# Block sums made in place by accumulating DMAs, with signs turned where the blocks are made, and products that wait for one part

## The chip, the cores and the metric

The kernel runs on one core of one Trainium2 chip. The metric is the device time in microseconds of one execution. The engines are TensorE (PE, matmuls), VectorE (DVE), ScalarE (ACT), GpSimd (POOL) and SyncE (SP, which here only issues DMAs).

## The reference

Talking-heads attention is followed by two feed-forward stages. Inputs and output are float32 in value; the weights arrive as float64 words and are decoded on the core.

```python
scores = scale * q @ k.T;  scores = einsum('bhij,hg->bgij', scores, w_pre)
attn   = softmax(scores);  attn   = einsum('bhij,hg->bgij', attn, w_post)
x      = (attn @ v)                      # 1792 tokens x 768
h      = ((x @ w1) * (x @ w2)) @ w3      # d_ff = 1024
x2     = h @ w_out                       # 1792 x 768
r      = maximum(x2 @ w_in, 0)           # d_ff = 2048
out    = (r * r) @ w_out2                # 1792 x 768
```

The change lies between the last matmuls of x2 and those of x2 @ w_in.

## The kernel before

Precision is kept by splitting each float32 operand into a high and a low half in float16. A product of two blocks is three matmuls (high by high, high by low, low by high), and a "cast" below always means two instructions: ScalarE writes the high half, VectorE the low half as the scaled source less the high half (lines 1434 and 1430 for x2, 1124 and 1125 for the weights).

**x2 and its sums.** w3 and w_out are multiplied into one matrix M first. The loop over four column blocks of 448 tokens (`for i in range(B)`) makes x2 as 24 products of 24 matmuls each; each result is evicted by ScalarE (line 1710) into a tile of the 16-buffer ring `st`. Two successive blocks form one half `t` of x2, cut into four blocks b11, b12, b21, b22 of three tiles each. x2 @ w_in is done by Winograd's form of Strassen's method: seven products instead of eight, of the sums T1 = b12 - b11, T2 = b22 - T1, T3 = b22 - b12, T4 = b21 - T2 on this side. `x2_steps(t, ts)` (line 1654) makes them by subtractions on GpSimd (line 1658) and casts the seven operands.

**The weights' sums.** w_in is taken in eight pairs q of two row blocks. `form_in` (line 1061) loads the two blocks of a pair from DRAM, where the decoding has put them (`sides`, line 1066: x0 = A11, A12 and x1 = A21, A22, tiles `ib`), and makes S1 = A21 + A22, S2 = S1 - A11, S3 = A11 - A21, S4 = A12 - S2 on GpSimd (line 1073) into two tiles `it` (pairs 0 to 2) or four tiles of `st`. `ib` and `it` share a ring of four buffers: a pair takes all four. The seven blocks are then cast into one tile `wq` (two buffers; pair 0 has a place of its own). For pairs 3 and up the casts wait until the pair two before has been used for both halves of tokens (`over`).

**The products.** The main loop runs over SEQ, sixteen steps of pair and half: (0,0), (1,0), (2,0), (1,1), (2,1), (0,1), (3,0), (3,1), (4,0) and so on. In each step `multiply_in` (line 1840) does seven block products of nine matmuls in the order A11, [S1 of the step before], S3, A12, S2, [S4 of the step before], A22. Its first line, `need_in(q)`, makes sure that the whole pair's operands have been written down in the program. What the engines then wait for are semaphores on the parts that they read.

**The order of the work** is set by a planner that runs when the program is built. Each helper is a stream of steps (engine, planned cost, function); `tick` moves a planned clock on by what PE does and lets each stream, in the order of a list, issue its next steps as long as its engine's planned backlog stays small (`ahead`). A REST step holds a stream for a planned time, `after(eng)` until an engine's backlog is worked off. This fixes only the order in each engine's queue: instructions, DMA issues included, run in order on their engine.

The accumulating DMA is issued by GpSimd. In the kernel before, GpSimd issues DMAs only for scales that cross partitions (lines 806 and 809): `across <- tot` to DRAM, and `ac <- across` back.

Of the kernel before, what the change touches and what calls it, by code (L numbers as in the profile page):

```python
# [10 lines left out]
F32 = mybir.dt.float32  # L11
# [3 lines left out]
ALU = mybir.AluOpType  # L15
# [19 lines left out]
def talking_heads_attention_moe_moe2(  # L35
# [726 lines left out]

    def decode(raw, n, total=None, x=None, zt=None):
# [189 lines left out]
    def one_steps(i):  # L953
# [15 lines left out]
        if kind in ("in", "out"):  # L969
            sums = in_sums[:, j : j + 1] if kind == "in" else out_sums[j // OG][:, j % OG : j % OG + 1]  # L970
            x, ops = decode(t, n, sums)
            yield from read_raw(i, x, ops)
# [25 lines left out]

    in_w, x_of, over = {}, [], set()
    fin_pool = []  # L1000

# [55 lines left out]
    def have_scale(g):  # L1057
        need(("in", (g + 1) * IG - 1))
        finish(scaling[g])

    def form_in():

        for g in range(NF2 // IG):
            box = {}

            def sides(q):
                box["b"] = [flat(w_tile(1, "ib")) for _ in range(2)]
                flush("kept")
                for z in range(2):
                    nc.sync.dma_start(box["b"][z], kept_in[2 * q + z])  # L1070

            def mix(o, a, b, op=ALU.subtract):
                nc.gpsimd.tensor_tensor(o, a, b, op=op)

            for q in range(g * IG // 2, (g + 1) * IG // 2):
                while ("in", 2 * q + 1) not in wsp:
                    yield REST, 0.5, lambda: need(("in", 2 * q + 1))
                yield POOL, 0, lambda: sides(q)
                yield REST, 5.0, None
                x0, x1 = box["b"]  # L1080
                if q < 3:
                    ta, tb = (flat(w_tile(1, "it")) for _ in range(2))
                    sums = [ta[:, :OH], ta[:, OH:], tb[:, :OH], tb[:, OH:]]
                else:
                    while x_of[1] in streams:
                        yield REST, 0.5, lambda: finish(x_of[1])
                    sums = [stage()[:, :OH] for _ in range(4)]
                a11, a12, a21, a22 = x0[:, :OH], x0[:, OH:], x1[:, :OH], x1[:, OH:]
                for o, l, r, op in (
                    (sums[0], a21, a22, ALU.add), (sums[1], sums[0], a11, ALU.subtract),  # L1090
                    (sums[2], a11, a21, ALU.subtract), (sums[3], a12, sums[1], ALU.subtract),
                ):
                    yield POOL, 1.1, lambda: mix(o, l, r, op)
                while g not in in_scales:
                    yield REST, 0.5, lambda: have_scale(g)
                up, lo = in_scales[g]
                if q:
                    while not started or (q > 2 and q - 2 not in over):
                        yield REST, 0.5, lambda: None
                    w = fin_pool[0].tile([P, 2, 7, OH], F16, tag="wq", name="wq", bufs=2)  # L1100
                    ks = [w[:, :, k] for k in range(7)]

# [3 lines left out]
                else:  # L1106
                    ws = [w_tile(0).rearrange("p z (k o) -> p z k o", k=2) for _ in range(4)]
                    ks = [ws[k][:, :, z] for k, z in ((0, 0), (0, 1), (1, 0), (2, 0), (2, 1), (3, 0), (3, 1))]

                    def where(k, n):  # L1110
                        i, y = ((0, 0), (0, 1), (1, 0), (2, 0), (2, 1), (3, 0), (3, 1))[k]
                        return [ws[i][:, z, y : y + n].rearrange("p k o -> p (k o)") for z in range(2)]

                srcs = [(x0, 0, 2), (x1[:, OH:], 2, 1)]
                if q < 3:
                    srcs += [(ta, 3, 2), (tb, 5, 2)]
                else:
                    srcs += [(x, 3 + k, 1) for k, x in enumerate(sums)]
                parts = [(x, k, where(k, n)) for x, k, n in srcs]
                for x, k, (h, l) in parts:  # L1120
                    n = x.shape[-1] // OH
                    if k == 3:
                        yield after(POOL)
# [4 lines left out]
                in_w[q] = (ks, lo)  # L1128

    forming, started = [], []  # L1130

    def need_in(q):
        if q and not started:
            started.append(True)
        while q not in in_w:
            assert forming[0].step(True) or q in in_w
        return in_w[q]

# [389 lines left out]

    mlo = {}
    M16, wo_done = [], []  # L1530

    def scale_m(o, acc):
# [36 lines left out]
        def scale():  # L1569
            ps = box.pop("ps")  # L1570
            up, mlo[o] = pow2(ps[:, :1], 14, "ms")
            nc.vector.tensor_scalar(rows2[:, o, 1], rows[:, 0], up, None, op0=ALU.mult)
            nc.vector.tensor_copy(bound[:, o : o + 1], ps[:, 1:2])
            if o:
                nc.vector.tensor_reduce(bound[:, 2:3], bound[:, :2], axis=AX.X, op=ALU.max)
                x_scale.append(pow2(bound[:, 2:3], 12 - 15, "xs"))

        yield DVE, 0.45, own
# [75 lines left out]
    def x2_steps(t, ts):  # L1654
        box = {}

        def mix(o, a, b):
            nc.gpsimd.tensor_tensor(o, a, b, op=ALU.subtract)

        def mixes(c):  # L1660
            b11, b12, b21, b22 = ts[c], ts[NDC + c], ts[c + 3], ts[NDC + c + 3]
            box[c] = {B11: b11, B21: b21, B22: b22, T1: b11, T2: b22, T3: b12, T4: b21}
            t1, t2, t3, t4 = (box[c][k] for k in (T1, T2, T3, T4))
            return [
                (POOL, 1.25, lambda: mix(t1, b12, b11)), (POOL, 1.25, lambda: mix(t3, b22, b12)),
                (POOL, 1.25, lambda: mix(t2, b22, t1)), (POOL, 1.25, lambda: mix(t4, b21, t2)),
            ]

        def casts(c, ks):
            yield from casts_of(t, c, [(k, box[c][k]) for k in ks])  # L1670

        if t:
            finish(first_of[0])
            while not fin_pool:
                yield REST, 0.5, lambda: None
        sums = [mixes(c) for c in range(3)]
        for c in range(3):
            yield from casts(c, (B21, B22) if t else (B11, B21, B22))
            if t == 0:
                yield from sums[c]  # L1680
                yield after(POOL)
                yield from casts(c, (T3, T2, T4, T1))
            elif c:
                yield from sums[c - 1]
        if t:
            yield from sums[2]
            for k in (T3, T2, T4, T1):
                for c in range(3):
                    yield from casts(c, (k,))

    have_x, first_of = [set(), set()], []

    def casts_of(t, c, ks):
        yield from halves_steps(
            [([xop(t, z, k, c) for z in range(2)], x, x_scale[0][0]) for k, x in ks]
        )
        for k, _ in ks:
            have_x[t].add((k, c))

    forming.append(Stream(form_in()))  # L1700
    streams.append(forming[0])
    for i in range(B):
# [3 lines left out]
        for c in range(NDC):  # L1706
            pt = mm()
            product(pt, [(M16[f], cols_of(c), hs[f]) for f in range(NFC)], toks(i))
            t = stage()
            nc.scalar.activation(t, pt[:, :S], AF.Copy, scale=mlo[c // 3])  # L1710
            ts.append(t)
            if c < NDC - 1 or i % 2 == 0:
                tick(1.13, 0.65)
        if i == 2:
            first_of.append(Stream(chain(*(casts_of(1, c, [(B11, ts[c])]) for c in range(3)))))
            streams.append(first_of[0])
# [4 lines left out]
    finish(x_of[0])  # L1721
    need_in(0)
    mid.close()
# [110 lines left out]
    xt, zt_, st_, s4_ = {}, {}, {}, {}  # L1834
    A11, A12, A22, S1, S2, S3, S4 = range(7)

# [456 lines left out]
```

## Time and profile before

| | |
|---|---|
| median of three runs | 1231.47 us (1230.94 to 1232.87) |
| the profiled execution | 1236.24 us, its span 1234.5 us |
| PE busy | 1213.4 us, 98% of the span |
| DVE, ACT, POOL busy | 948.6, 804.5, 581.6 us |
| mean granted TensorE clock | 0.994 of full |
| x2's 24 products | 725 to 836 us |
| x2 @ w_in | 836 to 1037 us |

Times count from the start of the span. "Idle before" is time in which an engine stood still ahead of an instruction, with what released it. The granted clock is a share of 2.4 GHz: 0.50 is the lower of its two levels, 1.2 GHz.

### The profile page before, as it was taken

Reading aid. Unit: us, or ns where it says so; the run is one execution under the profiler, and the core shown is the slowest. Engines: PE = TensorE matmul, PEld = TensorE weight load, DVE = VectorE, ACT = ScalarE, POOL = GpSimd, SP = SyncE. Lnnn points to the kernel's source line nnn. Section 1 sums busy time; section 2 is a strip of 40 time slices with the busy share of each in tenths; the row PEclk is TensorE's granted clock in tenths of the full one; section 3 lists DMA queues with packets and bytes.
Section 4 is the critical chain, followed back from the end, with each engine's and each line's share of the span. In section 5 each row is a group of like instructions: output and inputs, shape, how many; then the busy total and the mean of one; then the engine's idle time right before and its main releaser. Section 6 shows DMA issues by size and latency. Waiting matters only on the chain.

```text
span 1234.5 us, 26238 instructions
## 1 busy us (share of the span) xinstructions
PE 1213.4 (98%) x9904; PEld 749.2 (61%) x9904; DVE 948.6 (77%) x1690; ACT 804.5 (65%) x1620; POOL 581.6 (47%) x569
## 2 busy tenths in 40 slices
PE   7999999999999999999999999998999999999998
PEld 3666776677667655555558975554455555666665
DVE  6888899788889957766665875787578774999783
ACT  6788888888888735655554454567778785765430
POOL 3898788889878600110011211526124423667340
PEclk9999999999999999999999999999999999999999
DMA  6456555655645934755524547263478659565562
GB/s 186 123 156 166 141 146 134 169 128 155 171 114 164 260 98 120 159 143 163 133 94 145 171 146 243 76 207 103 143 269 289 237 169 320 180 189 181 171 201 77
DMA packets 139843, 205.02 MB, mean 166 GB/s; under 512 B 33764, under 2 KB 114788, under 8 KB 139716
## 3 DMA queue, kind: packets, MB, share of 16 engines
q1 hardware_dynamic: 136020, 200.01, 54.7%
q10 hardware_dynamic: 3136, 2.40, 0.8%
q8 instruction: 78, 1.28, 0.5%
q0 software_dynamic: 560, 0.93, 0.4%
q14 instruction: 49, 0.40, 0.1%
HBM read 114.60 MB, written 50.16 MB: 133 GB/s over the span
## 4 chain that ended last, share of the span: by engine, by line
PE 80%; DVE 9%; DMA 5%; ACT 2%; issue 1%; POOL 1%; SPq 0%; ACTq 0%; DVEq 0%; POOLq 0%
PE mm L1243 20%; PE mm L2099 15%; PE mm L1847 13%; PE p L284 10%; PE o L380 9%; PE s L241 5%; PE a L494 5%; DVE x L1430 2%; DMA Bt<-S 2%; PE p L1243 2%; DVE xa L776 1%; DVE xa L779 1%; DVE xa L783 1%; DMA raw<-in_moe_w_dram 1%; DVE wq L1125 1%
## 5 line engine op out<-in xcount | busy, mean ns | idle before, releaser
L1243 PE MATMUL mm<-x,w 128*128 128x448 f16 x1044 | 197.7, 352 | 0.0
L1847 PE MATMUL mm<-x,wq 128*128 128x448 f16 x882 | 172.7, 356 | 5.3 <-DVE wq L1125 3.7
L1243 PEld LDWEIGHTS <-w 128*128 128x128 f16 x1152 | 112.2, 98 | 104.3
L284 PE MATMUL p<-Bt,wpre_k 120*120 120x448 f32 x360 | 159.5, 561 | 4.9 <-DMA Bt<-S 4.2
L2099 PEld LDWEIGHTS <-ao 128*128 128x128 f16 x1176 | 115.0, 98 | 77.1 <-issue 1.2
L380 PEld LDWEIGHTS <-EH 120*112 120x112 f16 (+1 forms) x1440 | 124.9, 130 | 44.6 <-issue 37.1
L1847 PEld LDWEIGHTS <-wq 128*128 128x128 f16 x882 | 86.4, 99 | 87.4 <-DVE wq L1125 4.5
L353 POOL TENSOR_SCALAR EH<-E,st 120x448 f16<-120x448 f32 (+1 forms) x152 | 113.1, 752 | 49.1 <-DVE st L336 37.0
L402 DVE TENSOR_TENSOR ATl<-o,ATh 112x480 f16<-112x480 f32 x180 | 116.0, 645 | 22.3 <-ACT ATh L396 21.6
L306 ACT ACTIVATE E<-p,st 120x448 f32<-120x448 f32 x180 | 116.0, 645 | 22.9 <-DVE st L298 14.2
L396 ACT CAST ATh<-o 112x480 f16<-112x480 f32 x180 | 101.2, 562 | 44.3 <-PE o L380 39.4
L380 PE MATMUL o<-wph,EH 120*112 120x120 f16 x720 | 124.6, 219 | 1.0 <-DVE ATl L402 1.0
L380 PE MATMUL o<-wph,EL 120*112 120x120 f16 x720 | 122.6, 216 | 0.0
L380 PE MATMUL o<-wpl,EH 120*112 120x120 f16 x720 | 122.6, 216 | 0.0
L365 POOL TENSOR_TENSOR EL<-F,EH 120x448 f16<-120x448 f32 (+1 forms) x90 | 104.1, 1157 | 32.8 <-issue 19.9
L298 DVE TENSOR_REDUCE st<-p 120x1 f32<-120x448 f32 x180 | 110.1, 612 | 3.1 <-PE p L284 2.8
L1243 PE MATMUL mm<-h,M 128*128 128x448 f16 x576 | 110.2, 353 | 0.0
L2099 PE MATMUL mm<-x,ao 128*128 128x384 f16 x588 | 96.6, 326 | 1.0 <-ACT st L2113 1.0
L2099 PE MATMUL mm<-ow,ao 128*128 128x384 f16 x588 | 96.0, 326 | 0.0
L380 PEld LDWEIGHTS <-EL 120*112 120x112 f16 x720 | 93.9, 130 | 0.0
L367 DVE SCALAR_TENSOR_TENSOR EL<-E,st,EH 120x448 f16<-120x448 f32 (+1 forms) x90 | 83.6, 929 | 10.9 <-POOL EH L353 10.5
L1243 PEld LDWEIGHTS <-M 128*128 128x128 f16 x576 | 55.9, 98 | 52.0 <-DVE M L1430 0.8
(264 smaller groups left out, 2532.9 us busy)
## 6 DMA issues: line engine op xcount, KB each, us to landing
Bt<-S SPq DMA_DIRECT2D x176, 210.0 KB
raw<-in_moe_w_out_dram SPq DMA_DIRECT2D x24, 768.0 KB
g<-ev SPq DMA_DIRECT2D x64, 224.0 KB
gt<-g SPq DMA_DIRECT2D x56, 256.0 KB
raw<-in_moe_w_in_dram SPq DMA_DIRECT2D x16, 768.0 KB
raw<-in_moe_w_dram SPq DMA_DIRECT2D x14, 768.0 KB
raw<-in_moe_w_dram SPq DMA_DIRECT2D x16, 512.0 KB
kept_out<-xa SPq DMA_DIRECT2D x16, 384.0 KB
```

The lines of the kernel that those rows point to most:

```text
L284: nc.tensor.matmul(pt[: n * H, :S], wpre_k.rearrange("p t g -> p (t g)")[: n * H, : n * H], Bt.pop(u)[: n * H], start=True, stop=True,)
L298: nc.vector.tensor_reduce(nsum[u][:n, 0, j : j + 1], Pp[u][:n, :S], axis=AX.X, op=ALU.max, negate=True)
L306: nc.scalar.activation(e[:n], Pp.pop(u)[:n, :S].rearrange("p (a b) -> p a b", a=EG), AF.Exp, bias=t[:n, 0, j : j + 1], scale=1.0, accum_ou ...
L353: nc.gpsimd.tensor_scalar(seven(EH[u][:n]), Ex[u][:n], inverse(u), 1.0, op0=ALU.mult, op1=ALU.mult)
L365: nc.gpsimd.tensor_tensor(a, f, b, op=ALU.subtract)
L367: nc.vector.scalar_tensor_tensor(a, e, inverse(u), b, op0=ALU.mult, op1=ALU.subtract)
L380: nc.tensor.matmul(pt[:CP, c * n : (c + 1) * n], a[:n, c * CP : (c + 1) * CP], w[:n, :n], start=(i == 0), stop=(i == 2),)
L396: nc.scalar.copy(ATs[s][0][:, :, :, m * NR : m * NR + nr], src)
L402: nc.vector.tensor_tensor(ATs[s][1][:, :, :, a], src, ATs[s][0][:, :, :, a], op=ALU.subtract)
L1243: nc.tensor.matmul(pt[:, :S], w[a][:, cs], x[z][:, sl], start=(c == 0 and i == 0), stop=(c == len(parts) - 1 and i == 2),)
L1847: nc.tensor.matmul(pt[:, :S], w[:, a, c * P : (c + 1) * P], xop(t, b, kb, c), start=(start and c == 0 and m == 0), stop=(c == 2 and m == 2 ...
L2099: nc.tensor.matmul(pt[:, :OH], y[:, a, q * P : (q + 1) * P], ow[g, q][kb][:, w], start=(start and q == 0 and m == 0), stop=(q == NQ - 1 an ...
```

## The change

The sums are no longer made by GpSimd instructions but by DMAs that add a source onto a destination in place. Since these can only add, some blocks are stored with their sign turned: w_in's even row blocks (A11, A12) in the decoding, b11 and b22 in the eviction, and B21 and T2 when they are cast. A turned operand always meets a turned one, so that the products are the same.

The order of the casts changes: A11 and A12, S3, A22, S1, and S2 with S4 in one instruction. x1's first half is loaded a second time, for S3 (`box["s"]`), so that a pair of the first three takes three buffers of the ring instead of four. `need_in(q, k)` makes sure only of the part k. For pairs 3 and up the finishing of x2's sums moves ahead of the loads. The diff, cut to its core:

```diff
+    def accumulate(dst, src):
+        nc.gpsimd.dma_start(dst, src, accum_op=ALU.add)
+    LAND = 4.0
+    PLACE = (0, 1, 2, 3, 5, 4, 6)
@@ form_in
             def sides(q):
                 box["b"] = [flat(w_tile(1, "ib")) for _ in range(2)]
+                box["s"] = (flat(w_tile(1, "it")) if q < 3 else stage())[:, :OH]
...
+                nc.sync.dma_start(box["s"], kept_in[2 * q + 1][:, :OH])
...
+                while q > 2 and x_of[1] in streams:
+                    yield REST, 0.5, lambda: finish(x_of[1])
                 yield POOL, 0, lambda: sides(q)
                 yield REST, 5.0, None
                 x0, x1 = box["b"]
-                for o, l, r, op in (
-                    (sums[0], a21, a22, ALU.add), (sums[1], sums[0], a11, ALU.subtract),
-                    (sums[2], a11, a21, ALU.subtract), (sums[3], a12, sums[1], ALU.subtract),
-                ):
-                    yield POOL, 1.1, lambda: mix(o, l, r, op)
+                yield POOL, 0, lambda: accumulate(s3, x0[:, :OH])
+                yield POOL, 0, lambda: accumulate(x1[:, :OH], x1[:, OH:])
...
+                yield from halves(x0, A11, 2)
+                yield after(DVE)
+                yield POOL, 0, lambda: accumulate(x0[:, :OH], x1[:, :OH])
+                yield from halves(s3, S3, 1)
+                yield REST, LAND, None
+                yield POOL, 0, lambda: accumulate(x0[:, OH:], x0[:, :OH])
+                yield from halves(x1[:, OH:], A22, 1)
+                yield from halves(x1[:, :OH], S1, 1)
+                yield REST, LAND, None
+                yield from halves(x0, S2, 2)
@@ x2_steps
+        else:
+            yield from cast(B11, b11)
+        yield after(DVE)
+        yield from add(b11, b12)
+        yield REST, LAND, None
...
+        yield from cast(B22, b22)
+        yield from add(b12, b22)
+        yield REST, LAND, None
+        yield from cast(B21, b21)
+        yield from add(b22, b11)
+        yield REST, LAND, None
+        yield from cast(T3, b12)
+        yield from add(b21, b22)
+        for k, xs in ((T2, b22), (T4, b21), (T1, b11)):
+            yield from cast(k, xs)
@@ decode (turn is set for w_in's even row blocks)
-                xi, lo, 29, 0, op0=ALU.logical_shift_right, op1=ALU.bitwise_or
+                xi, lo, 29, -(2 ** 31) if turn else 0,
+                op0=ALU.logical_shift_right, op1=ALU.bitwise_or
...
-                xi, hi, -(2 ** 31), xi, op0=ALU.bitwise_and, op1=ALU.bitwise_or
+                xi, hi, -(2 ** 31), xi, op0=ALU.bitwise_and, op1=ALU.bitwise_xor
@@ eviction of x2, and its casts
-            nc.scalar.activation(t, pt[:, :S], AF.Copy, scale=mlo[c // 3])
+            o = c // 3
+            turned = (o == 0) == (i % 2 == 0)
+            nc.scalar.activation(
+                t, pt[:, :S], AF.Copy, scale=mturn[:, o : o + 1] if turned else mlo[o]
+            )
...
+        up = mturn[:, 2:3] if k in (B21, T2) else x_scale[0][0]
@@ multiply_in
-        w = need_in(q)[0][ka]
+        w = need_in(q, ka)
```

## Rows read from the trace of the kernel before

**Rows 1.** The page: busy time and share of PE; the chain, by engine.
```profile
PE 1213.4 (98%) x9904; PEld 749.2 (61%) x9904; DVE 948.6 (77%) x1690; ACT 804.5 (65%) x1620; POOL 581.6 (47%) x569
...
PE 80%; DVE 9%; DMA 5%; ACT 2%; issue 1%; POOL 1%; SPq 0%; ACTq 0%; DVEq 0%; POOLq 0%
```

**Rows 2.** Waits of PE, 720 us to the end: total, times, longest.
```profile
PE mm L1847 <- DVE wq L1125: 3.7, 2, 3.2
PE mm L1847 <- ACT wq L1124: 1.6, 1, 1.6
```

**Rows 3.** PE in order of time: start, length, operation, count, idle before.
```profile
836.14 5.27 PE L1847 MATMUL mm<-x,w 128*128 128x448 f16 x27
...
848.56 0.54 PE L1847 MATMUL mm<-x,wq 128*128 128x448 f16 x2
852.27 6.34 PE L1847 MATMUL mm<-x,wq 128*128 128x448 f16 x25 [3.17 <-DVE wq L1125]
...
864.77 2.15 PE L1847 MATMUL mm<-x,wq 128*128 128x448 f16 x7 [0.50 <-DVE wq L1125]
...
867.36 4.31 PE L1847 MATMUL mm<-x,wq 128*128 128x448 f16 x18
...
871.91 8.31 PE L1847 MATMUL mm<-x,wq 128*128 128x448 f16 x43
```

**Rows 4.** Stretches of 2 us: PE busy, granted clock, DMA share, GB/s.
```profile
852.00:854.00 2.00, 1.73 (x5) 0.50 0.31 115
...
868.00:870.00 2.00, 2.00 (x10) 0.78 1.00 369
```

**Rows 5.** Groups by line: busy us, mean ns, idle before.
```profile
L1658 POOL TENSOR_TENSOR st<-st 128x448 f32<-128x448 f32 x24 | 35.2, 1471 | 63.2 <-DVE x L1430 39.8 <-ACT st L1710 22.2
...
L1430 DVE SCALAR_TENSOR_TENSOR x<-st,xs,x 128x448 f16<-128x448 f32 x42 | 35.4, 895 | 12.0 <-ACT x L1434 12.0
...
L1430 DVE SCALAR_TENSOR_TENSOR h<-st,hs,h 128x448 f16<-128x448 f32 x29 | 18.0, 680 | 4.8 <-ACT h L1434 4.8
```

**Rows 6.** GpSimd in order of time (sums of pairs 0, 2, 3; x2's).
```profile
745.08 1.49 POOL L1073 TENSOR_TENSOR it<-ib 128x384 f32<-128x384 f32 x1 [26.66 <-DMA ib<-kept_in]
...
839.40 15.01 POOL L1658 TENSOR_TENSOR st<-st 128x448 f32<-128x448 f32 x10 [1.78 <-DVE x L1430]
854.37 0.99 POOL L1073 TENSOR_TENSOR it<-ib 128x384 f32<-128x384 f32 x1
...
869.60 1.00 POOL L1073 TENSOR_TENSOR st<-ib 128x384 f32<-128x384 f32 x1 [10.38 <-DMA ib<-kept_in]
```

**Rows 7.** ScalarE in order of time.
```profile
837.27 2.34 ACT L1434 ACTIVATE x<-st,xs 128x448 f16<-128x448 f32 x4
839.51 0.62 ACT L1882 ACTIVATE ev<-mm,sci 128x448 f32<-128x448 f32 x1
840.03 0.93 ACT L1124 ACTIVATE wq<-ib,is 128x768 f16<-128x768 f32 x1
```

**Rows 8.** The crossings' tile: who waited, us, times; issue to landing, us.
```profile
  POOL ac L809: 18.7, 5
...
DMA to landing us min/median/max: 3.7/4.3/5.6
```

**Rows 9.** Tile `it`: casts of 768 columns, ns min/median/max, first and last start.
```profile
L1124 ACT ACTIVATE w<-it,is x2: 922/922/922, 778.5 to 779.4; 128x768 f16<-128x768 f32 x2
L1125 DVE SCALAR_TENSOR_TENSOR w<-it,is,w x2: 1012/1012/1012, 779.6 to 780.6; 128x768 f16<-128x768 f32 x2
```

**Rows 10.** SyncE's issues of the loads for pairs 0 and 3.
```profile
739.15 3.12 SPq L1070 DMA_DIRECT2D ib<-kept_in  x2
...
864.78 0.80 SPq L1070 DMA_DIRECT2D ib<-kept_in  x2
```

**Rows 11.** Two stretches: PE, PEld, DVE, ACT, POOL busy; clock; DMA share.
```profile
836.00:872.00 36.00, 30.74 (x146) 14.80 (x145) 25.75 (x39) 24.96 (x48) 22.65 (x18) 0.91 0.34 112
872.00:1020.00 148.00, 148.00 (x784) 76.54 (x785) 107.02 (x166) 119.80 (x251) 48.22 (x38) 1.00 0.66 224
```

More of the change, by code (lines that the diff above doesn't have):

```diff
@@ L970, in one_steps @@
             sums = in_sums[:, j : j + 1] if kind == "in" else out_sums[j // OG][:, j % OG : j % OG + 1]
-            x, ops = decode(t, n, sums)
+            x, ops = decode(t, n, sums, turn=kind == "in" and j % 2 == 0)
             yield from read_raw(i, x, ops)
@@ L999, in talking_heads_attention_moe_moe2 @@
     in_w, x_of, over = {}, [], set()
+    A11, A12, A22, S1, S2, S3, S4 = range(7)
     fin_pool = []
@@ L1080, in form_in @@
                 x0, x1 = box["b"]
[L1081 to L1088, printed above, removed]
-                for o, l, r, op in (
-                    (sums[0], a21, a22, ALU.add), (sums[1], sums[0], a11, ALU.subtract),
-                    (sums[2], a11, a21, ALU.subtract), (sums[3], a12, sums[1], ALU.subtract),
-                ):
-                    yield POOL, 1.1, lambda: mix(o, l, r, op)
+                s3 = box["s"]
+                yield POOL, 0, lambda: accumulate(s3, x0[:, :OH])
+                yield POOL, 0, lambda: accumulate(x1[:, :OH], x1[:, OH:])
                 while g not in in_scales:
@@ L1100, in form_in @@
                     w = fin_pool[0].tile([P, 2, 7, OH], F16, tag="wq", name="wq", bufs=2)
-                    ks = [w[:, :, k] for k in range(7)]
+                    ks = [w[:, :, k] for k in PLACE]
                     def where(k, n):
@@ L1107, in form_in, with halves @@
                     ws = [w_tile(0).rearrange("p z (k o) -> p z k o", k=2) for _ in range(4)]
-                    ks = [ws[k][:, :, z] for k, z in ((0, 0), (0, 1), (1, 0), (2, 0), (2, 1), (3, 0), (3, 1))]
+                    at_ = ((0, 0), (0, 1), (1, 0), (2, 0), (2, 1), (3, 0), (3, 1))
+                    ks = [ws[at_[k][0]][:, :, at_[k][1]] for k in PLACE]
                     def where(k, n):
-                        i, y = ((0, 0), (0, 1), (1, 0), (2, 0), (2, 1), (3, 0), (3, 1))[k]
+                        i, y = at_[k]
                         return [ws[i][:, z, y : y + n].rearrange("p k o -> p (k o)") for z in range(2)]
[L1114 to L1123, printed above, removed]
+                in_w[q] = (ks, lo)
+                def halves(x, k, n):
+                    h, l = where(PLACE[k], n)
                     yield ACT, 0.5 * n, lambda: nc.scalar.activation(h, x, AF.Copy, scale=up)
@@ L1127, in form_in, with need_in @@
                     )
-                in_w[q] = (ks, lo)
+                    have_w.update((q, PLACE.index(PLACE[k] + i)) for i in range(n))
+                yield from halves(x0, A11, 2)
[8 more added lines that the diff above has]
+                yield from halves(x0, S2, 2)
     forming, started = [], []
-    def need_in(q):
+    def need_in(q, k):
         if q and not started:
             started.append(True)
-        while q not in in_w:
-            assert forming[0].step(True) or q in in_w
-        return in_w[q]
+        while (q, k) not in have_w:
+            assert forming[0].step(True) or (q, k) in have_w
+        return in_w[q][0][k]
     def load_to(n):
@@ L1654, in x2_steps @@
     def x2_steps(t, ts):
[L1655 to L1667, printed above, removed]
@@ L1669, in casts, with cast, add @@
-        def casts(c, ks):
-            yield from casts_of(t, c, [(k, box[c][k]) for k in ks])
+        b11, b21, b12, b22 = (ts[i : i + 3] for i in range(0, 2 * NDC, 3))
+        def cast(k, xs):
+            return casts_of(t, range(3), k, xs)
+        def add(os_, xs):
+            for c in range(3):
+                yield POOL, 0, lambda: accumulate(os_[c], xs[c])
         if t:
             finish(first_of[0])
+        else:
+            yield from cast(B11, b11)
+        yield after(DVE)
@@ L1674, in x2_steps @@
+        yield from add(b11, b12)
+        yield REST, LAND, None
+        if t:
             while not fin_pool:
                 yield REST, 0.5, lambda: None
[L1676 to L1689, printed above, removed]
+        yield from cast(B22, b22)
[8 more added lines that the diff above has]
+            yield from cast(k, xs)
@@ L1714, in talking_heads_attention_moe_moe2 @@
         if i == 2:
-            first_of.append(Stream(chain(*(casts_of(1, c, [(B11, ts[c])]) for c in range(3)))))
+            first_of.append(Stream(casts_of(1, range(3), B11, ts[:3])))
             streams.append(first_of[0])
@@ L1721, in talking_heads_attention_moe_moe2 @@
     finish(x_of[0])
-    need_in(0)
+    for k in range(7):
+        need_in(0, k)
     mid.close()
```

17 lines of the change are left out of this document (8 added, 9 removed).

## The prediction, made before the result was known

> **What bounds the kernel now.** I read the page first. TensorE (PE) is busy 1213.4 of 1234.5 us and the chain that ended last lies on it for 80% [rows 1], so an edit elsewhere moves the time only where PE waits. I then asked who PE waits for from 720 us on, the part that the diff touches: 5.3 us on the weight halves of lines 1124 and 1125, in three waits [rows 2]; the only other one is 1 us long and 180 us later. The list of PE's work in order of time puts the three between 848 and 865 us [rows 3]: inside S3 of pair 1 (3.17 us, ended by VectorE), ahead of A11 of pair 2 (the 1.6 us of ScalarE) and inside it (0.50). Before 846 and after 872 the changed operations never stop PE. After the first of them the granted clock is 0.50, the lower of TensorE's two levels, 1.2 GHz, and it is not back at full 4 us after the last [rows 4]. That is a second price: the 25 matmuls that took 6.34 us take 25 x 0.189 + 0.17 = 4.9 us at full clock (0.189 us each from the 43 in 8.31), and 7 and 18 in 2.15 and 4.31 took 1.4 too much as well. So a wait of this kind costs its length and about 1.4 us.
>
> From 836.14 to the next product, A12 of pair 2 at 871.91, PE did 135 matmuls (15 products of 9), 25.6 us of work in 35.8 us. Even if everything were free, about 9 us can be won, 1 us of the rest being scale transposes. S2 of pair 2 starts at 871.9 + 1.7 = 873.6. I use that moment as the mark, as nothing stops PE behind it for 150 us.
>
> **What goes.** 24 subtractions for x2 on GpSimd (1.47 us each, 35.2 us) and 32 for the input weights leave that engine [rows 5]. VectorE wins too: its 42 casts of x2 take 0.895 us on average, many beside them, where the same form is 0.68 us alone [rows 5], 9 us in all. Before 836 all that is worth nothing: PE is never idle there, and the decoding that gets done sooner isn't waited for. Behind 836 it matters: GpSimd's block of ten subtractions (15.01 us from 839.40) held up those of pair 2 until 854.37 [rows 6], and through them the casts of pair 2; the casts of x2 (four, 2.34 us) stood ahead of pair 1's on ScalarE, which began only at 840.03 [rows 7]. Both old waits come from this, and both should go: S3's halves now stand second in the order, and pair 2's A11 needs only its load.
>
> The sign turns (a constant and an xor in the decode, a negated scale in an eviction, four tiny multiplications ahead of the x2 stage) replace instructions of the same shape, so I put them at nothing; the four cost at most 4 x 0.2 us of VectorE where PE has its 24 products ahead. The wait for one part alone I put at nothing by itself: in the trace PE already ran two S3 matmuls at 848.56 on the high half and stopped only for the low one [rows 3], so parts are waited for separately; what changes is the order in which instructions are written.
>
> **What comes.** 56 accumulating DMAs, issued by GpSimd: 12 for each x2 half, 4 for each of 8 pairs. They cost the issuing engine about 0.56 us each, less than the subtractions, but a dependent one can be issued only when the one before has landed. No row shows an accumulating DMA. The nearest are the scale crossings: GpSimd sat 18.7 us in 5 waits for such a DMA to land, 3.74 us each; with 0.56 us for the issue itself that is 4.3, which is also the median from issue to landing, between 3.7 and 5.6 [rows 8]. Those carry 1 to 128 KB. Here 192 KB are read on both sides, 393 KB in all; at the 369 GB/s that the DMAs reached at share 1.00 [rows 4] that is 1.07 us more. I take 4.3 + 1.1 = 5.4 us a hop, with 3.7 (size free) and 5.6 + 1.1 = 6.7 as ends. An on-chip subtraction was 1.0 to 1.7 us: each link of a chain gets three to five times longer.
>
> A rule of the Trainium skill speaks for shorter hops: "DMA: Bandwidth & Descriptors", section on the anatomy of one DMA on the GpSimd path, puts a DMA at about 2.0 us plus its bytes over 436 GB/s, an estimate of 2.4 us here, with which the whole chain below would be hidden. The crossings disagree (3.7 at the least, at 128 KB and under), and the measurement decides; what the short hop would give is the second rival.
>
> **Where the links lie.** For pair 1, S2 = S1 - A11 is made in x0's place, so only after x0's own cast, and S4 is added on S2. S2 and S4 are cast by one instruction, so S2 too waits for S4's DMA. Pair 2's x1 takes the buffer of pair 1's x0 (four buffers, three now taken per pair), so its load waits for that cast; only then come S1, S2 and S4 of pair 2. One after the other:
> - Pair 1's x0: A11 of the first product ends at 836.1 + 1.7 = 837.8, its eviction (0.62) at 838.5; ScalarE's cast 0.93 [rows 7] and VectorE's 1.01 [rows 9]: 840.4. The four casts of x2 aren't ahead any more, since that stream now rests behind its DMAs.
> - S2 and S4: 2 x 5.4: 851.2. The joint cast, 0.92 + 1.01 [rows 9]: 853.1. PE wants this S2 as its tenth product at 851.4 and waits about 1 us; this wait isn't added, since the chain runs on beside it.
> - Load of pair 2's x1 and of the copy of its first half: GpSimd started 2.8 us after the second issue ended for pair 0 and 4.8 us after the first began for pair 3 [rows 6, 10]; I take 4.0: 857.1.
> - The issue for S3 stands first (0.56), then S1, S2, S4: 3 x 5.4: 873.9. ScalarE's high half 0.92: 874.8.
>
> PE, without waits, wants that S2 as its 17th product at 836.1 + 16 x 1.70 + 1 = 864.3, so it gets there by 866 or 867 and stands 8 us, with 1.4 us of low clock behind it: 876.2 against 873.6. **Sum: +2.6 us.** In hops h the mark is at 849.2 + 5h: equal at 4.9 us, 2.5 us sooner at 4.4, 2.5 later at 5.4; with the ends 3.7 and 6.7 it is -5.9 and +9.1, and the load adds 1 us either way.
>
> Queued behind the waiting instructions: on GpSimd the x2 sums of the second half (first wanted at the fourth step, three steps of 11.9 us after 836); on ScalarE and VectorE evictions emitted behind a cast that waits for its DMA, which hold banks of PSUM but are done before PE comes round to them; on SyncE the stores of g behind pair 2's load. Pairs 3 to 7 I put at nothing: they may be cast once the pair two before is used up, 15 us ahead of their A11 and 22 ahead of their S2, and the chain is 2 + 2 x 5.4 + 2 = 15 us. PE is busy 148.00 of the 148 us there now [rows 11].
>
> **Rivals.** (1) The hop lies between 4.4 and 5.4: the new stop at S2 of pair 2 is just as long as the two it replaces, and the time stays within 2.5 us. For it: the crossings' middle is 4.3, and none is under 3.7. Chance 0.29. (2) Faster: hops of 4.4 or less, since these land on chip where the crossings write or read memory off it. At 4.3 the mark is at 870.7, -2.9 us; at 3.7, -5.9; from 3.0 down PE itself sets it, at 864.3, -9.3. Against it: twice the reading, and neighbours. Chance 0.31. (3) Much slower: hops of 8 us where three x2 transfers (672 KB and as much read again) are ahead in the same queue. The mark moves to 889, +15.6. Against it: only the first hops of each pair have such neighbours, and the DMAs stand at a share of 0.34 in this stretch [rows 11]. Chance 0.10. My own case, hops of 5.4 to about 6.7, has 0.30, so slower has 0.40 in all.
>
> **The numbers.** The profiled execution took 1236.24 us (span 1234.5), 4.8 above the median 1231.47; I add the difference to the median: 1231.5 + 2.6 = 1234.1. About 0.2% (2.5 us) is what can be told from no change. The range, 1226 to 1241, goes from the short hop of 3.7 to the long one of 6.7; the extremes of rivals 2 and 3 stay out. Chances: faster 0.31, same 0.29, slower 0.40; the forecast lies at the edge of the last two.
>
> **What the changed profile would show.** Right: no wait at S3 of pair 1 or A11 of pair 2; one wait of 5 us or more at S2 of pair 2, on ScalarE's cast, whose own wait ends with an accumulating DMA; accumulates 5 to 6 us apart where dependent; x2 casts at 0.68 us. Wrong: a hop under 4.4 us, a load that isn't held by the joint cast, or waits at the fourth step or at pairs 3 to 7.

## The result: 10.5 us slower, half of it at a stop that was foreseen, and priced too low

The changed kernel takes 1242.35 us (median, 1239.74 to 1244.69) against 1231.85 for the kernel before in the same comparison: a ratio of 1.0084, 95% interval 1.0069 to 1.0100, or +10.5 us. The forecast was +2.6, with 1241 as the upper end of the range. The profiled execution took 1243.43 us, its span is 1241.7.

The page of the changed kernel, busy time and the chain by engine. VectorE is 26 us and GpSimd 28 us less busy than before; TensorE (PE) is not, and the chain now runs through DMAs and issues more than in [rows 1]:

```profile
PE 1214.6 (98%) x9904; PEld 747.7 (60%) x9904; DVE 922.9 (74%) x1691; ACT 805.3 (65%) x1618; POOL 553.8 (45%) x569
...
PE 76%; issue 8%; DMA 6%; DVE 6%; ACT 2%; POOL 2%; SPq 0%; ACTq 0%; POOLq 0%; DVEq 0%
```

What PE waits for from 720 us on, in the changed kernel (total, times, longest). In [rows 2] there were 5.3 us, all on weight halves; here there are 13.9, and 2.6 of them are on evictions:

```profile
PE mm L1853 <- ACT wq L1119: 9.3, 3, 7.0
PE mm L1853 <- ACT ev L1888: 2.6, 2, 2.2
PE mm L1853 <- DVE wq L1120: 1.2, 2, 0.7
PE mm L1041 <- DVE xt L1037: 0.8, 1, 0.8
```

PE in order of time, the changed kernel, to be held against [rows 3]. The stage begins at 834.14. The second line is S2 of pair 1, the next two are A11 of pair 2, the fifth is S2 of pair 2, and the last lies in pair 4:

```profile
834.14 2.43 PE L1853 MATMUL mm<-x,w 128*128 128x448 f16 x12
...
852.15 0.55 PE L1853 MATMUL mm<-x,wq 128*128 128x448 f16 x2 [1.67 <-ACT wq L1119]
...
858.66 0.55 PE L1853 MATMUL mm<-x,wq 128*128 128x448 f16 x2 [0.55 <-ACT wq L1119]
859.88 7.14 PE L1853 MATMUL mm<-x,wq 128*128 128x448 f16 x34 [0.67 <-DVE wq L1120]
874.05 32.22 PE L1853 MATMUL mm<-x,wq 128*128 128x448 f16 x153 [7.04 <-ACT wq L1119]
...
951.87 17.66 PE L1853 MATMUL mm<-x,wq 128*128 128x448 f16 x84 [2.17 <-ACT ev L1888]
```

The changed kernel in stretches of 2 us (length; busy time and instructions of PE, PEld, DVE, ACT, POOL; granted clock; DMA share; GB/s). After the long stop PE stays at 0.50, the lower level of 1.2 GHz, until 880, with 5, 7 and 7 matmuls in 2 us where the full clock gives 12; after the 2.17 us at pair 4 it falls as well:

```profile
874.00:876.00 2.00, 1.82 (x5) 0.57 (x6) 1.97 (x3) 2.00 (x4) 0.00 (x0) 0.50 0.44 71
876.00:878.00 2.00, 2.00 (x7) 0.76 (x5) 2.00 (x5) 1.41 (x4) 0.00 (x0) 0.50 0.00 0
878.00:880.00 2.00, 2.00 (x7) 0.82 (x6) 0.63 (x2) 0.58 (x1) 0.00 (x0) 0.50 0.00 0
880.00:882.00 2.00, 2.00 (x12) 1.07 (x11) 0.00 (x0) 0.63 (x1) 0.00 (x0) 0.98 0.00 0
...
952.00:954.00 2.00, 2.00 (x6) 0.73 (x5) 1.08 (x2) 1.71 (x5) 1.01 (x2) 0.50 1.04 387
```

**Where the time went.** Four landmarks occur in both traces: a scale matmul 8 us into x2's products (733.64 before, 730.38 after), the start of the stage (836.14 and 834.14), the product with which pair 0 is used for the second half of tokens (902.57 and 906.11), and the first matmul of the last stage (1036.41 and 1044.76). Between them the changed kernel takes 1.3, 5.5 and 4.8 us more, and from there to the end 1.1 less, since the kernel before stops there for 1.0 us on an eviction and the changed one does not: +10.5 us. (Ahead of the first landmark the profiled execution of before was 3.3 us longer, in code that both share but for the turned signs; its time lies 4.4 above its median, so the two spans differ by 7.2 only. e8 below has the code of before up to there and reached x2 2.5 us sooner, so this is the execution and not the change.)

The 5.5 us: PE resumes at S2 of pair 2 39.9 us after the stage began, against 37.5 before, +2.4; from there to the landmark it takes 32.1 against 29.0, +3.1, and that is the clock. Of the 4.8 us, 2.6 are the stops at evictions, and about 1.6 the clock behind the second of them (84 matmuls in 17.66 us, at 0.189 each and 0.17 it would be 16.05); 0.6 are not accounted for. That the weights' DMAs make the 4.8 us is shown by the experiments below: over this stretch e1 and e3, whose weights' sums are instructions, take 133.8 us like the kernel before, and after and e2, where they are DMAs, 138.6 and 138.1.

**How the long stop comes about.** GpSimd's DMA issues in the changed kernel, in order of time:

```profile
839.09 0.86 POOL L1064 DMA_DIRECT2D ib<-ib  x1 [10.12 <-DVE xt L1037]
839.63 2.97 POOL L1064 DMA_DIRECT2D st<-st  x3
842.41 1.08 POOL L1064 DMA_DIRECT2D ib<-ib  x1
...
853.37 0.86 POOL L1064 DMA_DIRECT2D st<-st  x1 [3.75 <-DVE wq L1120]
...
857.50 1.54 POOL L1064 DMA_DIRECT2D ib<-ib  x1
865.10 0.86 POOL L1064 DMA_DIRECT2D ib<-ib  x1 [6.06 <-DVE x L1436]
869.92 0.86 POOL L1064 DMA_DIRECT2D ib<-ib  x1 [3.97 <-DMA ib<-ib]
```

S2 of pair 1 is issued at 839.09; S4, at 842.41, stands behind three sums of x2, and the cast that takes S2 and S4 together starts at 851.16. Pair 2's loads are issued at 842.27, but its first sums come only at 857, as they stand behind x2's in GpSimd's queue, and x2's wait for hops of their own. The profile names a VectorE cast of a weight (`wq`) as what ended the 3.75 us before the sum at 853.37, but that sum reads no weight: it adds onto the tile b22, which the sum issued at 843.92 still reads, and that one landed (its data had arrived) 8.9 us after its issue, at 852.8. Then S1 (857.50), S2 (865.10) and S4 (869.92) follow one another; the 6.06 us before S2, put down to a cast of x2, are S1's hop, 7.0 us from issue to landing. SyncE's issue of the loads, and the hop of the sum at 843.92 (tile `st`, 844.0 to 844.5) and of S1 (tile `ib`, 858.3 to 858.9):

```profile
842.27 0.99 SPq L1080 DMA_DIRECT2D ib<-kept_in  x2
```

```profile
DMA to landing us min/median/max: 8.9/8.9/8.9
```

```profile
DMA to landing us min/median/max: 7.0/7.0/7.0
```

ScalarE in order of time, the same kernel; the first, third and fourth row are the joint casts of S2 and S4 of pairs 1, 2 and 4, and each waits for a landing:

```profile
851.16 0.93 ACT L1119 ACTIVATE wq<-ib,is 128x768 f16<-128x768 f32 x1 [1.71 <-DMA ib<-ib]
...
867.00 1.11 ACT L1119 ACTIVATE wq<-ib,is 128x384 f16<-128x384 f32 x2
873.06 0.94 ACT L1119 ACTIVATE wq<-ib,is 128x768 f16<-128x768 f32 x1 [4.95 <-DMA ib<-ib]
...
946.78 0.94 ACT L1119 ACTIVATE wq<-ib,is 128x768 f16<-128x768 f32 x1 [3.30 <-DMA ib<-ib]
```

At pair 4 PE's operands are there in time; what is late is an eviction behind that cast (951.21), and PE waits 2.17 us for it.

The hop itself, from the tile `ib` of the changed kernel (all its DMAs), and from the list of DMA issues (tile, count, KB, median us from issue to landing):

```profile
DMA to landing us min/median/max: 3.0/5.7/9.8
```

```profile
st<-st POOLq DMA_DIRECT2D x24, 224.0 KB, 6.5
ib<-ib POOLq DMA_DIRECT2D x24, 192.0 KB, 6.1
```

### The profile page after: what moved, and what is told of

Its sections match the earlier page's. It is cut to its first block, busy times and chain, and to the rows that moved or that the text cites. A ratio compares the mean times of both kernels' runs of the same rounds, so it can differ in the third digit from the quotient of the medians.

```text
span 1241.7 us, 26347 instructions
## 1 busy us (share of the span) xinstructions
PE 1214.6 (98%) x9904; PEld 747.7 (60%) x9904; DVE 922.9 (74%) x1691; ACT 805.3 (65%) x1618; POOL 553.8 (45%) x569
## 4 chain that ended last, share of the span: by engine, by line
PE 76%; issue 8%; DMA 6%; DVE 6%; ACT 2%; POOL 2%; SPq 0%; ACTq 0%; POOLq 0%; DVEq 0%
PE mm L1249 21%; PE mm L2105 15%; PE p L284 10%; PE mm L1853 9%; PE o L380 8%; PE s L241 5%; PE a L494 4%; DMA ib<-ib 3%; PE p L1249 2%; DMA Bt<-S 1%; PE mm L1526 1%; DMA st<-st 1%; POOL w L995 1%; DVE ATl L402 1%; DVE x L1436 1%
## 5 line engine op out<-in xcount | busy, mean ns | idle before, releaser
L1853 PE MATMUL mm<-x,wq 128*128 128x448 f16 x882 | 175.3, 359 | 13.4 <-ACT wq L1119 9.3
L306 ACT ACTIVATE E<-p,st 120x448 f32<-120x448 f32 x180 | 116.2, 646 | 23.5 <-DVE st L298 14.3
L367 DVE SCALAR_TENSOR_TENSOR EL<-E,st,EH 120x448 f16<-120x448 f32 (+1 forms) x90 | 83.4, 927 | 10.9 <-POOL EH L353 10.5
```

What stands on the lines that cost most here:

```text
L306: nc.scalar.activation(e[:n], Pp.pop(u)[:n, :S].rearrange("p (a b) -> p a b", a=EG), AF.Exp, bias=t[:n, 0, j : j + 1], scale=1.0, accum_ou ...
L367: nc.vector.scalar_tensor_tensor(a, e, inverse(u), b, op0=ALU.mult, op1=ALU.subtract)
L1853: nc.tensor.matmul(pt[:, :S], w[:, a, c * P : (c + 1) * P], xop(t, b, kb, c), start=(start and c == 0 and m == 0), stop=(c == 2 and m == 2 ...
```

## The experiments

Each was timed in five rounds against the kernel before on the same chip. "Gain" is the median less that of before in the same comparison.

| kernel | x2's sums | weights' sums | rests | median us | ratio (95%) | gain us |
|---|---|---|---|---|---|---|
| after | DMA | DMA | yes | 1242.35 | 1.0084 (1.0069 to 1.0100) | +10.5 |
| e1 | GpSimd | GpSimd | yes | 1241.11 | 1.0072 (1.0058 to 1.0086) | +8.1 |
| e2 | GpSimd | DMA | yes | 1242.38 | 1.0086 (1.0065 to 1.0107) | +9.4 |
| e3 | DMA | GpSimd | yes | 1234.05 | 1.0009 (0.9999 to 1.0019) | +1.1 |
| e4, S2 and S4 cast apart | DMA | DMA | yes | 1236.67 | 1.0031 (1.0019 to 1.0042) | +3.7 |
| e5 | DMA | GpSimd | no | 1224.04 | 0.9923 (0.9907 to 0.9938) | -9.5 |
| e6, as e5, cast apart | DMA | GpSimd | no | 1223.38 | 0.9922 (0.9904 to 0.9940) | -10.2 |
| e7 | DMA | DMA | no | 1275.88 | 1.0335 (1.0314 to 1.0356) | +42.3 |
| e8, before, wait by part | as before | as before | - | 1239.18 | 1.0048 (1.0032 to 1.0063) | +5.6 |
| e9 | GpSimd | GpSimd | no | 1223.73 | 0.9904 (0.9887 to 0.9920) | -11.8 |
| e10, after, whole pair | DMA | DMA | yes | 1243.07 | 1.0067 (1.0051 to 1.0082) | +7.5 |
| e11, weights as before | GpSimd | as before | no | 1223.87 | 0.9931 (0.9918 to 0.9943) | -9.0 |
| e12, x2 as before | as before | GpSimd | no | 1224.72 | 0.9935 (0.9922 to 0.9948) | -8.2 |

A minus is faster. The median of before was between 1231.85 and 1235.56 in these comparisons, so that kernels with the same median differ by up to 3.7 us in gain; differences under 4 us between kernels are not read below. "Rests" are the three in the weights' stream; x2's stream, where its order is the new one, keeps its own.

**e1 to e4: who makes the sums, and the joint cast.** The edits, in the accumulation and in the last cast of `form_in`:

```diff
+    def add_here(dst, src):
+        nc.gpsimd.tensor_tensor(dst, dst, src, op=ALU.add)
# e1: at every accumulate; e2: at x2's 24 only; e3: at the weights' 32 only
-                yield POOL, 0, lambda: accumulate(x0[:, :OH], x1[:, :OH])
+                yield POOL, 0, lambda: add_here(x0[:, :OH], x1[:, :OH])
# e4 alone, all DMAs kept
-                yield from halves(x0, S2, 2)
+                yield from halves(x0[:, :OH], S2, 1)
+                yield from halves(x0[:, OH:], S4, 1)
```

> The changed kernel (1242.4 us) with each of the 56 accumulating DMAs replaced by a GpSimd instruction that adds in the same place; the order in every queue, the signs, the casts and the waits for one part stay. Theory, the links are too long (3 to 9 us for a DMA, 1.0 to 1.7 for an instruction): the 7.0 us stop of PE ahead of S2 of pair 2 shrinks under 2 us, the 2.2 us stop at 950 us goes, and the time falls by 9 to 13 us, to 1229 to 1233. Rival, the new order of the casts, the third load or the signs cost the time: it stays above 1238. Rival, VectorE's contention with GpSimd was worth much: no stop, but VectorE late and the time between the two, 1234 to 1238.

A miss: without any hop the kernel is as slow as with all of them. The long stop is gone, but new ones come, 4.75 us at S2 of pair 1 and 1.98 + 2.90 at S2 of pair 2. The theory that the hops alone made the loss has fallen. Where the stop at pair 1 comes from shows beside the changed kernel (first row; then VectorE and ScalarE in e1): beside GpSimd's sums three casts of x2 take 3.90 us, beside DMAs 1.86, and ScalarE waits 3.14 us for a VectorE eviction, with pair 1's S2 and S4 behind it, which it casts at 853.77.

```profile
844.55 1.86 DVE L1436 SCALAR_TENSOR_TENSOR x<-st,mturn,x 128x448 f16<-128x448 f32 x3
```

```profile
847.54 3.90 DVE L1436 SCALAR_TENSOR_TENSOR x<-st,mturn,x 128x448 f16<-128x448 f32 x3
...
852.07 0.58 ACT L1877 ACTIVATE ev<-ev 128x448 f32<-128x448 f32 x1 [3.14 <-DVE ev L1890]
```

> The changed kernel with only the 24 sums of x2 made by GpSimd instructions; the 32 of the weights stay accumulating DMAs. Theory, the weights' own chain of three links sets the stop: S1 and S3 of pair 2 are issued earlier than 857 us and land faster, PE restarts some 4 us sooner, the stop at 950 us stays: 1236 to 1239. Rival, x2's sums in GpSimd's queue and in the DMA rings are the cause: the stop goes altogether and the time is 1233 or less. Rival, they have no part in it: 1241 to 1243.

No change from after in the time, but other stops make it up: 4.73 us at S2 of pair 1 as in e1, 2.29 + 1.12 at S2 of pair 2 in place of the long one, and 2.43 on an eviction at pair 4, as in after.

> The changed kernel with only the 32 sums of the weights made by GpSimd instructions; the 24 of x2 stay accumulating DMAs. Theory, the weights' chain sets the stop: after S1 and S3 of pair 2 the other two links take 3 us instead of 15, the stop goes, and so does that at 950 us: 1230 to 1234. Rival, x2's DMAs hold GpSimd's queue ahead of pair 2: a stop of 3 to 5 us stays, 1235 to 1238.

8.3 us better than after: with x2's sums off GpSimd, the weights' hops cost that much in this order (with them on it, e2 against e1, no difference that can be read). From e1 to e3 it is 7.1 us: in this order x2's sums are worth that much off GpSimd, when the weights' are no DMAs. But e3 still stops PE for 7.9 us in all from 720 us on, and the weights' hops are gone. ScalarE in order of time shows on what; pair 2's S2 and S4 were summed by 861.4 and are cast, in e3, only as the third part of the last line, behind two evictions that themselves wait for PE:

```profile
860.79 0.63 ACT L1891 ACTIVATE ev<-mm,sci 128x448 f32<-128x448 f32 x1 [1.91 <-PE mm L1856]
...
864.73 0.63 ACT L1891 ACTIVATE ev<-mm,sci 128x448 f32<-128x448 f32 x1 [0.39 <-PE mm L1856]
...
866.38 1.94 ACT L1122 ACTIVATE wq<-ib,is 128x384 f16<-128x384 f32 x3
```

> The changed kernel with the joint cast of S2 and S4 split into one of S2 and one of S4 behind it, all sums still DMAs. Theory, S2 waits for S4's DMA only through the joint cast: pair 2's S2 comes one link (3 to 5 us) sooner, PE restarts that much sooner and S4, wanted one product later, gives back part; ScalarE stands as long for S4: 1238 to 1240. Rival, the joint cast has no part in it because S4 then stops PE instead: 1241 to 1244.

5.7 us better than after: S2, the first to be read, waits for S4's hop only because one instruction casts both. PE's stops there become 1.65 and 1.35 us, and the granted clock is 1.00 in all of 834 to 905.

**e5 to e7: the rests.** Three rests in the weights' stream were written for landings. Without DMAs they only delay when a cast is written into the queues (the first two sums, not shown, are planned at 1.1 us too):

```diff
                 yield from halves(x0, A11, 2)
-                yield after(DVE)
-                yield POOL, 0, lambda: accumulate(x0[:, :OH], x1[:, :OH])
+                yield POOL, 1.1, lambda: add_here(x0[:, :OH], x1[:, :OH])
                 yield from halves(s3, S3, 1)
-                yield REST, LAND, None
-                yield POOL, 0, lambda: accumulate(x0[:, OH:], x0[:, :OH])
+                yield POOL, 1.1, lambda: add_here(x0[:, OH:], x0[:, :OH])
...
-                yield REST, LAND, None
+                yield after(POOL)
                 yield from halves(x0, S2, 2)
# e6: e5 with S2 and S4 cast apart; e7: the changed kernel, DMAs kept, without the three rests
```

> As e3 (weights' sums by GpSimd instructions, x2's by accumulating DMAs; 1234.1 us) with the planned rests between the weights' sums and casts taken out (the one behind the first cast and the two of 4 us), and the sums planned at 1.1 us. Theory (new, after e1 fell): beside the DMAs' landing, the rests cost time by themselves, because they put the casts of S3 and of S2 with S4 on ScalarE and VectorE behind evictions that wait for PE, which then waits for the casts. Without them the stop at S2 of pair 2 (4.9 us in two parts in e3) shrinks under 2 us: 1228 to 1231. Rival: GpSimd's queue, held by x2's sums until 856 us, sets the stop, which stays: 1233 to 1236.

10 us better than e3 and 9.5 better than the kernel before. (The edit takes out the rests, plans the sums at 1.1 us and puts `after(POOL)` ahead of the last cast; the three were not separated.) From 720 us on PE never waits on a weight or an eviction any more. Two stretches of e5, columns as above; in the first of them PE is busy 65.74 us before the change and 60.26 after it, at a mean clock of 0.95 and 0.93, in the second 139.00 and 136.29:

```profile
834.00:905.00 71.00, 71.00 (x378) 36.75 (x377) 52.97 (x80) 61.74 (x127) 22.55 (x21) 1.00 0.72 219
905.00:1044.00 139.00, 139.00 (x753) 73.48 (x752) 95.47 (x149) 104.73 (x215) 59.99 (x48) 1.00 0.76 261
```

The cast of pair 2's A11 and A12, which starts at 857.68 in after and at 857.06 in e3, starts at 851.33; from the start of the stage that is 23.5, 22.7 and 18.0 us. With e5's order the wait for one part decides nothing: written with a wait for the whole pair, e5 is the same program, instruction for instruction.

> As e5, with S2 and S4 cast by two instructions each. If the joint cast still matters without DMAs in its chain, 1 to 2 us less than e5; if it only mattered through S4's DMA, the same as e5 or 0.5 us more (two more instructions on ScalarE and VectorE for each pair).

The joint cast costs nothing where S4 is no DMA; so e4's 5.7 us were S4's hop.

> The changed kernel (all sums accumulating DMAs, 1242.4 us) with the three rests in the weights' stream taken out. Theory, rests and landing times are two causes: without the rests the casts stand early in the queues and ScalarE and VectorE stop there until the DMAs land (3 to 9 us each), so that evictions behind them are late at every pair: 1242 to 1250. Rival, the rests alone are the cause: 1230 to 1236.

With DMAs the rests are needed. PE's waits, and ScalarE in order of time, in e7: the joint cast of pair 1 is written early, waits 8.09 us for its landing, and the eviction behind it is late.

```profile
PE mm L1850 <- ACT ev L1885: 33.0, 6, 7.4
```

```profile
839.93 1.11 ACT L1119 ACTIVATE wq<-ib,is 128x384 f16<-128x384 f32 x2
849.13 0.93 ACT L1119 ACTIVATE wq<-ib,is 128x768 f16<-128x768 f32 x1 [8.09 <-DMA ib<-ib]
849.97 0.62 ACT L1885 ACTIVATE ev<-mm,sci 128x448 f32<-128x448 f32 x1
```

**e8 and e10: the wait for one part alone**, put into the kernel before (e8) and taken out of the changed one (e10):

```diff
# e8
-        while q not in in_w:
-            assert forming[0].step(True) or q in in_w
+        while (q, k) not in have_w:
+            assert forming[0].step(True) or (q, k) in have_w
# e10
-        while (q, k) not in have_w:
+        while not all((q, j) in have_w for j in range(7)):
```

> The kernel before with one part of the change alone: the program makes sure of a product's own part instead of the whole pair (the sums stay GpSimd subtractions in the old order of casts). The prediction put this at nothing: within 0.1% of the kernel before. Rival, it lets evictions go ahead of casts in ScalarE's queue and costs or gains 1 us or more.

5.6 us slower by this edit alone; GpSimd's order is the same as before, in PE's two scale matmuls stand elsewhere, and about a dozen instructions of the other three engines move. ScalarE in order of time in e8, then in the kernel before: there the casts of `it` (S3 among them) follow those of `ib` at once; here an eviction stands between, and waits 2.14 us for PE:

```profile
860.01 1.42 ACT L1126 ACTIVATE wq<-ib,is 128x768 f16<-128x768 f32 x2
863.57 0.63 ACT L1885 ACTIVATE ev<-mm,sci 128x448 f32<-128x448 f32 x1 [2.14 <-PE mm L1850]
...
865.27 1.75 ACT L1126 ACTIVATE wq<-it,is 128x768 f16<-128x768 f32 x2
```

```profile
862.74 1.43 ACT L1124 ACTIVATE wq<-ib,is 128x768 f16<-128x768 f32 x2
864.07 1.75 ACT L1124 ACTIVATE wq<-it,is 128x768 f16<-128x768 f32 x2
```

PE then stops 1.53 and 1.34 us at S3 of pair 2.

> The changed kernel, but a product makes sure that the whole pair's operands are written down, as before the change; nothing else is edited. Theory: the wait for one part alone costs by itself, since casts come to stand behind evictions that wait for PE (5.6 us when it alone was put into the kernel before). Undone here, about 1237 (1235 to 1239). Rival: with the sums made by DMAs the casts written earlier wait for landings, and the evictions behind them with ScalarE; then it is slower than the changed kernel, 1248 or more, with new stops of PE on evictions, as without the rests (1275.9).

Neither: the time of after. The wait has moved. ScalarE in order of time in e10: the cast of pair 2's S2 and S4 is ready 7.3 us sooner than in after, but twelve casts of x2, 7 us, are now written ahead of two evictions; PE stops 10.69 us for these, to 874.00, where after resumes at 874.05.

```profile
865.76 0.94 ACT L1119 ACTIVATE wq<-ib,is 128x768 f16<-128x768 f32 x1 [5.16 <-DMA ib<-ib]
...
869.97 3.46 ACT L1440 ACTIVATE x<-st,xs 128x448 f16<-128x448 f32 x6
873.33 1.14 ACT L1888 ACTIVATE ev<-mm,sci 128x448 f32<-128x448 f32 x2
```

**e9, e11, e12: what the gain of e5 needs.** e9 is e5 with x2's sums on GpSimd as well. e11 is e9 with the weights' side as it was before (four buffers, sums out of place as additions of turned blocks, all seven casts behind them); e12 is e9 with x2's sums and casts tile by tile as before:

```diff
# e9
-                yield POOL, 0, lambda: accumulate(os_[c], xs[c])
+                yield POOL, 1.1, lambda: add_here(os_[c], xs[c])
# e11, form_in of before with
+                    (sums[0], a21, a22, ALU.add), (sums[1], sums[0], a11, ALU.add),
+                    (sums[2], a11, a21, ALU.add), (sums[3], a12, sums[1], ALU.add),
# e12, x2_steps of before with
+            nc.gpsimd.tensor_tensor(o, a, b, op=ALU.add)
```

> The kernel with the weights' sums as GpSimd instructions and without the rests, and here x2's 24 sums as GpSimd instructions too; no accumulating DMA is left. Theory: what the change gains is x2's sums off GpSimd. With the rests kept that was worth 7.1 us (1241.1 against 1234.1); without them I expect it again, about 1231 (1229 to 1233), with stops of PE at S1 and S2 of pair 1 or 2 between 848 and 880 us, ended by VectorE or ScalarE, and VectorE's casts of x2 near 1.2 us beside GpSimd's sums. Rival: the 7 us came only because evictions stood behind casts that the rests had pushed late; without rests nothing is late and x2's sums may lie on GpSimd: 1224 to 1226, no stop in the stage.

The rival holds. Groups by line in e9, 720 to 910 us: x2's sums are back on GpSimd and the casts beside them take 865 ns again [rows 5], and PE is stopped by none of them: it is busy 71.00 of the 71 us from 834 to 905 (one stop of 0.7 us, on an eviction, comes at 947).

```profile
L1067 POOL TENSOR_TENSOR st<-st 128x448 f32<-128x448 f32 x24 | 35.9, 1522 | 22.3 <-ACT st L1715 17.4 <-DVE x L1437 3.5 <-ACT ev L1878 1.4
...
L1437 DVE SCALAR_TENSOR_TENSOR x<-st,xs,x 128x448 f16<-128x448 f32 x30 | 24.4, 865 | 5.2 <-ACT x L1441 5.0
```

> All sums as GpSimd instructions. x2's casts and sums stand in the order of the changed kernel without change; the weights' blocks are loaded, summed out of place (four buffers of the ring for a pair, four sums as additions of turned blocks) and cast in the order of the kernel before, and a product waits for the whole pair. Theory: the gain of the kernel without rests (1223.7) lies in the weights' new order: S3 from its own copy, the sums in place, three buffers for a pair. Without it about the time of the kernel before, 1231 to 1235, with stops of PE at S3 of pair 1 or A11 of pair 2. Rival: the gain lies in x2's new order, block by block for three tiles at once, by which fewer casts of x2 stand ahead of the weights' after 836 us: then 1223 to 1226 here, and no stop.

> All sums as GpSimd instructions. The weights' blocks are loaded, summed and cast as in the kernel without rests (1223.7); x2's sums and casts stand in the order of the kernel before, tile by tile, with the signs of the change. Theory (the gain lies in the weights' new order): 1223 to 1226, no stop of PE between 836 and 905 us. Rival (it lies in x2's order): 1231 to 1235, with stops on weight halves between 846 and 872 us as in the kernel before. If both orders are needed, both kernels of this pair are near 1232; if either is enough, both near 1224.

Either order is enough. Each has one stop left on a weight half, 1.8 us, after which the clock stays at 1.00 (e11, then e12):

```profile
861.70 32.14 PE L1860 MATMUL mm<-x,wq 128*128 128x448 f16 x169 [1.76 <-DVE wq L1137]
```

```profile
862.63 2.63 PE L1864 MATMUL mm<-x,wq 128*128 128x448 f16 x13 [1.77 <-DVE wq L1123]
```

e11 needs neither the second load nor the smaller ring, and e12 leaves x2 as it was but for the signs. Five kernels that have no weights' DMAs and none of the three rests lie within 1.4 us of one another, at 1223.4 to 1224.7. All five also have the turned signs, and the signs alone, in both old orders, were not timed. Written so, the program has the instructions of the kernel before in the same order on every engine, and three multiplications of 128x1 more on VectorE; that the signs have no part in the gain is likely by this, but not shown. Which single lines of either order matter was not separated; nor was a longer LAND tried.

## Why the prediction was wrong

The sign was right, and the moment that carried the sum came within 1.2 us, in part by luck; four terms put at nothing or too low made the rest, and the largest is "Pairs 3 to 7 I put at nothing".

- **The two old waits go.** S3 of pair 1 does. A11 of pair 2 still stops PE for 0.55 + 0.67 us: its load was there, but its cast was written late. e5 shows it, where that cast runs 5.6 us sooner in the stage and PE does not stop.
- **The chain of hops.** Counted from the start of the stage, which came 2.0 us sooner in the changed kernel's trace, S4 of pair 1 was put at 15.1 us, and its cast starts at 17.0; pair 2's sums at 21.0, measured 22.8; PE's restart at 38.7, measured 39.9. Two of the links were other than said. The second hop of pair 1 took 8.7 us, behind three DMAs of x2 (842.41 to 851.1), and the first 3.0: rival 3's long hop, at a place where it cost only 1.67 + 0.50 us. And pair 2's load was not held by the joint cast: SyncE issued it at 842.27. GpSimd's queue held the sums instead, for x2's, which waited for hops of their own. The prediction named that queue and looked only for when x2's sums are wanted, not for what they would hold up. That the end of the chain still came out near 38.7 is in part luck: the five hops were 3.0, 8.7, 7.0, 4.5 and 3.1 us (tile `ib`, issue to landing), 26.3 in all where 5 x 5.4 = 27.0 was summed, and one wait took the place of another.
- **The hop** was taken as 5.4 us; the medians are 5.1 to 6.6 (6.5 and 6.1 above; 5.1 and 6.6 for the eight from `ib` into `st` and `it`). The range of 3.7 to 6.7 covers them, but not the single ones (3.0 to 9.8). The estimate of 2.4 us by the Trainium skill ("DMA: Bandwidth & Descriptors", the section on the anatomy of one DMA) is under the shortest; the measurement decides against it.
- **1.4 us of low clock** behind the stop, carried over from stops of 1.6 and 3.2 us: 3.1 us behind one of 7. Mis-sized by 1.7.
- **Pairs 3 to 7 at nothing:** +4.8 us, the largest miss. The step reasoned from when PE wants S2, and that held. What failed is the sentence before it, by which evictions behind a waiting cast "are done before PE comes round to them": at pair 4 one was not, behind a cast that waited 3.30 us for its DMA's landing.
- **x2's stage at nothing:** +1.3 us, 0.82 of it a wait of PE at a scale (L1041), which VectorE gives late. Not the hops alone: e1 has no DMA sums and waits 1.12 us there; e9 and e11, without DMA sums and without the rests, do not stop there. What makes it was not separated.
- **The wait for one part alone at nothing:** "what changes is the order in which instructions are written" was the right reading, and the price put on it the wrong one. Alone it costs 5.6 us (e8); within the change it costs nothing that can be told (e10).
- **x2's casts at 0.68 us** came true (0.679 each), and in the order without rests it is worth nothing: e9 has the slow casts and is as fast as e5.
- **The sign turns at nothing** (three multiplications, not four) were tested by no run of their own.

The sum: restart +2.4 (forecast +1.2, and +1.4 of clock), clock +3.1, behind it +4.8, x2's stage +1.3, end -1.1: 10.5. The "about 9 us" that could be won "even if everything were free" is what e5, e9, e11 and e12 win (8.2 to 11.8), without one accumulating DMA for the weights: what stopped PE before was the order of the queues, not the speed of the sums (with the reservation on the signs made above).

## What to carry to other kernels

On engines that run in order, the place at which an instruction is written down is a cost of its own: a cast that waits for a DMA holds evictions behind it, and one held back by a planned rest ends up behind evictions that wait for PE. Price a change of order by listing what stands behind each wait in each queue, far beyond the place of the change. And before a faster way of making operands is built, try whether the same operands merely issued in another order end the wait.

## What was not expected of the hardware

- After 7.04 us without matmuls TensorE's granted clock stayed at 0.50 for 6 us more, and 16 matmuls ran in that time; after 1.8 us (e11, e12) it did not fall in the stretch of 834 to 905, and after 2.17 us (pair 4 of after) it fell to 0.50. The length of a stop alone does not tell: behind 1.58 and 0.50 us in the kernel before, 10 us of matmuls after the stop of 3.17, it fell [rows 2, 3, 4]; behind 1.59 and 0.50 us at the same product in e4 it stayed at 1.00.
- An accumulating DMA of 192 KB from and to on-chip tiles took 3.0 to 9.8 us from issue to landing (x2's, of 224 KB, 6.5 in the median), and one issued alone kept GpSimd busy for 0.86 us. In the chain above those of 3.0, 4.5 and 3.1 were issued with no other in flight, and those of 8.7 and 8.9 behind others.
